# Four column tiles per unit of the expert layer, in one PSUM tile of two banks

## The chip, the cores and the metric

The kernel runs on one core of a Trainium2 chip. The metric is the device time of one execution in microseconds (us). The core's engines are PE (matmul; its weight loads are PEld), DVE (vector), ACT (activation functions), POOL (a second vector engine) and SP, which only issues transfers here. Each has its own queue and works through it in order.

## What is computed

Four sequences of 768 steps pass through a delta rule with 8 heads of width 48; its output, 3072 rows of 384, is the input x of an expert layer with 2048 hidden columns and a rational function in place of an activation:

```python
# delta rule, per batch and head
y[t] = q[t] @ state
state += beta[t] * outer(kn[t], v[t] - kn[t] @ state)
# expert layer on x = all heads' y, side by side
h = x @ w_in                      # [3072, 384] @ [384, 2048]
P = a0 + a1*h + a2*h*h + a3*h*h*h
Q = 1 + |b0|*|h| + |b1|*h*h
out = (P / (Q + 1e-6)) @ w_out    # [3072, 2048] @ [2048, 384]
```

w_in and w_out come as float64; the kernel converts them itself.

## The kernel before

**Stages.** The sequences are cut into 12 chunks of 64 steps (NCH). For a chunk the delta rule is turned into block matmuls over all heads: `front`, `middle`, `back` and `ahead` (lines 898 to 967) each have eight steps j, and `attention` (969) calls them for four different chunks at once, so that chunk c+1 is solved while chunk c+4 is loaded. A chunk gives 256 rows of x (64 steps of four sequences), which `tokens` (731) transposes and scales and `scalars` (757) gives its factors.

**A unit.** The expert layer takes a chunk's 256 rows against w_in in 8 units of two tiles of 128 hidden columns, 96 units in all, each with 2 x 256 = 512 numbers in each of 128 partitions. A product is made of three passes of 16-bit halves (PASSES). A unit n goes through four functions:

- `hidden` (802): 18 matmuls on PE (L810) into the PSUM tile ph. Its tag "h" in the pool ps_h has two buffers of one bank each (line 87), so that unit n+1 can be made while unit n is read.
- `numerator` (820): ACT makes a3*h + a2 (L827) and |b1*h| (L829) from ph; DVE makes u = h * that (L830), the denominator's part w (L832) and u's next step (L834), all three reading ph. L834 is the last reader of ph. ACT takes |w| (L833). In some units, by_pool (line 836), POOL adds a0 (L838).
- `quotient` (841): ACT makes 1/Q by Ln and Exp (L845, L846). DVE multiplies (L851, or L849 in by_pool units) and forms the rest for the low half (L852 and L856; in by_pool units POOL does the latter, L854). POOL writes the low half of g (L857).
- `accumulate` (860): 12 matmuls on PE (L872) add g @ w_out to two PSUM tiles po, the first eight from g's high half, the last four from the low half that POOL writes. After a chunk's last unit the result is scaled and stored.

by_pool holds for units 0, 4, 5 and 6 of chunks 2 to 10, 36 of 96.

**Order.** The loop at line 1010 calls, for each n, numerator(n), quotient(n-1), one attention step, accumulate(n-2) and hidden(n+1). The scheduler of the framework then lays the instructions out on each engine's queue by its own timeline; what stands in the queues is not the order of the calls.

**Weights.** `load_in` and `load_out` (338, 356) bring w_in and w_out in pieces through `to_f32` (318): one transfer, |.| on ACT (L325), a clamp on POOL (L326), three integer steps on DVE (L327, L334). They find one scale for each unit of two tiles. The staging tiles share the buffers of the expert layer's u, r and w (tags mu, mr, mw; three each) and of g (mg; three). Half of the weights (GRP = 4 units) are ready before the first unit, the rest is converted while the first four units run.

## Time and profile before

| | |
|---|---|
| time, median of 3 runs (lowest, highest) | 870.12 us (870.11, 876.16) |
| span of the profiled execution | 875.0 us |
| mean granted PE clock in it | 0.886 |
| busy: PE, PEld, DVE, ACT, POOL | 629.4, 494.5, 797.9, 550.9, 469.5 us |
| instructions | 23209 |
| first numerator step (L830) | at 151.9 us |
| L830 of the first unit of chunks 2, 9, 10, 11 | at 307.0, 745.4, 790.6, 831.7 us |

The profile is of one execution, whose span is 875.0 us, 4.9 us over the median of the runs. A row of a group gives line, engine, operation, output and inputs by tile names, shapes, count, then busy time in all and the mean of one in ns, then the engine's idle time ahead of them and what ended it. A row of the timeline begins with the start and the duration in us. On DVE an instruction's duration reaches into the next one's start by some 0.08 us, so that what it costs the queue is the time from start to start.

### The profile page before, as it was taken

Reading aid. Unit: us, or ns where it says so; the run is one execution under the profiler, and the core shown is the slowest. Engines: PE = TensorE matmul, PEld = TensorE weight load, DVE = VectorE, ACT = ScalarE, POOL = GpSimd, SP = SyncE. Lnnn points to the kernel's source line nnn. Section 1 sums busy time; section 2 is a strip of 40 time slices with the busy share of each in tenths; the row PEclk is TensorE's granted clock in tenths of the full one; section 3 lists DMA queues with packets and bytes.
Section 4 is the critical chain, followed back from the end, with each engine's and each line's share of the span. In section 5 each row is a group of like instructions: output and inputs, shape, how many; then the busy total and the mean of one; then the engine's idle time right before and its main releaser. Section 6 shows DMA issues by size and latency. Waiting matters only on the chain. (4 is left out here: it accounts for less than half of the span.)

```text
span 875.0 us, 23209 instructions
## 1 busy us (share of the span) xinstructions
PE 629.4 (72%) x9264; PEld 494.5 (57%) x9264; DVE 797.9 (91%) x1561; ACT 550.9 (63%) x1025; POOL 469.5 (54%) x430
## 2 busy tenths in 40 slices
PE   0230444875787688698778879788788878898885
PEld 0120344664565576576556667666566657676553
DVE  5999899899999789999989999999999898898996
ACT  4765675656466386585566678567576664868574
POOL 7655664537236447656646755654756444363622
PEclk9755556886999799899989989999999998999998
DMA  8987986679965987988689489597683824300000
GB/s 236 247 185 156 224 175 111 122 132 168 177 121 93 180 142 131 182 142 162 118 155 170 82 162 152 90 194 116 128 172 63 166 46 65 68 1 19 1 19 18
DMA packets 466507, 111.46 MB, mean 127 GB/s; under 512 B 431328, under 2 KB 463072, under 8 KB 466400
## 3 DMA queue, kind: packets, MB, share of 16 engines
q1 hardware_dynamic: 464224, 108.83, 66.8%
q8 instruction: 72, 1.18, 0.6%
q10 hardware_dynamic: 2176, 1.17, 0.4%
q14 instruction: 35, 0.29, 0.1%
HBM read 40.47 MB, written 26.23 MB: 76 GB/s over the span
## 5 line engine op out<-in xcount | busy, mean ns | idle before, releaser
L872 PE MATMUL po<-w_out,mg 128*128 128x384 f16 x1152 | 220.6, 339 | 42.2 <-POOL mg L857 33.7
L810 PE MATMUL ph<-xT,w_in 128*128 128x256 f16 x1728 | 221.5, 283 | 33.3 <-DVE mu L834 30.2
L810 PEld LDWEIGHTS <-w_in 128*128 128x128 f16 x1728 | 172.6, 102 | 70.5 <-DVE mu L834 22.4
L857 POOL TENSOR_TENSOR mg<-mu,mr 128x512 f16<-128x512 f32 x96 | 131.9, 1374 | 107.8 <-DVE mu L856 52.5
L872 PEld LDWEIGHTS <-mg 128*128 128x128 f16 x1152 | 109.7, 101 | 118.1 <-POOL mg L857 42.8
L827 ACT ACTIVATE mu<-ph,coef,msc 128x512 f32<-128x512 f32 x96 | 74.1, 772 | 50.4 <-POOL mg L857 17.3
L833 ACT ACTIVATE mw<-mw 128x512 f32<-128x512 f32 x96 | 60.3, 630 | 64.0 <-DVE mw L832 63.7
L852 DVE SCALAR_TENSOR_TENSOR mw<-mw,msc,mg 128x512 f32<-128x512 f32 x96 | 88.4, 922 | 0.4
L410 PEld LDWEIGHTS <-kbd 128*128 128x128 f16 x1680 | 61.7, 105 | 38.8 <-issue 36.2
L830 DVE TENSOR_TENSOR mu<-ph,mu 128x512 f32<-128x512 f32 x96 | 65.5, 683 | 17.1 <-ACT mr L829 13.4
L854 POOL TENSOR_TENSOR mu<-mu,mw 128x512 f32<-128x512 f32 x36 | 50.1, 1390 | 54.3 <-DVE mw L852 30.8
L832 DVE SCALAR_TENSOR_TENSOR mw<-mr,msc,ph 128x512 f32<-128x512 f32 x96 | 70.6, 736 | 0.0
L410 PE MATMUL pu<-z,ebd 128*128 128x48 f16 x1728 | 56.5, 188 | 19.4 <-DVE z L234 11.8
L834 DVE SCALAR_TENSOR_TENSOR mu<-mu,msc,ph 128x512 f32<-128x512 f32 x96 | 70.4, 733 | 0.0
L845 ACT ACTIVATE mr<-mw,msc 128x512 f32<-128x512 f32 x96 | 69.0, 720 | 1.8
L410 PEld LDWEIGHTS <-ebd 128*128 128x128 f16 x1728 | 55.3, 100 | 22.4 <-issue 20.9
L829 ACT ACTIVATE mr<-ph,msc 128x512 f32<-128x512 f32 x96 | 65.4, 681 | 0.0
L851 DVE SCALAR_TENSOR_TENSOR mg<-mu,msc,mr 128x512 f16<-128x512 f32 x60 | 61.5, 1024 | 2.3 <-ACT mr L846 2.3
L838 POOL TENSOR_SCALAR mu<-mu,msc 128x512 f32<-128x512 f32 x36 | 31.3, 869 | 56.3 <-DVE mu L834 50.2
L846 ACT ACTIVATE mr<-mr 128x512 f32<-128x512 f32 x96 | 60.2, 628 | 1.2
L856 DVE SCALAR_TENSOR_TENSOR mu<-mu,msc,mw 128x512 f32<-128x512 f32 x60 | 57.6, 960 | 0.2
L232 POOL TENSOR_TENSOR mm<-m,mm 128x1024 f16<-128x1024 f32 x12 | 30.3, 2527 | 44.2 <-ACT mm L228 36.0
(201 smaller groups left out, 1295.9 us busy)
## 6 DMA issues: line engine op xcount, KB each, us to landing
wsi<-in_moe_w_in_dram SPq DMA_DIRECT2D x24, 256.0 KB, 5.2
xdk<-kn SPq DMA_DIRECT2D x24, 256.0 KB, 3.6
kbd<-tk SPq DMA_DIRECT2D x24, 256.0 KB, 5.4
gd<-g SPq DMA_DIRECT2D x24, 256.0 KB, 3.4
wso<-in_moe_w_out_dram SPq DMA_DIRECT2D x32, 192.0 KB, 4.1
xdq<-kn SPq DMA_DIRECT2D x24, 256.0 KB, 3.4
mbd<-mm SPq DMA_DIRECT2D x24, 256.0 KB, 5.0
wc<-img SPq DMA_DIRECT2D x24, 256.0 KB, 4.9
```

Of the source, the lines that this page charges most:

```text
L410: nc.tensor.matmul(dst[p][:, h], head(bd, lp, p * H + h), head(rt, rp, p * H + h), start=start and n == 0 and h == 0, stop=stop and n == l ...
L810: nc.tensor.matmul(ph[:, i], w_in[:, f2, wp, cc, i * P : (i + 1) * P], x[:, xp, cc], start=k == 0, stop=k == 3 * NCC - 1,)
L827: nc.scalar.activation(u, ph, AF.Identity, scale=A3, bias=a2)
L829: nc.scalar.activation(z, ph, AF.Abs, scale=B1)
L830: nc.vector.tensor_mul(u, ph, u)
L832: nc.vector.scalar_tensor_tensor(out=w, in0=z, scalar=B0, in1=ph, op0=ALU.add, op1=ALU.mult)
L834: nc.vector.scalar_tensor_tensor(out=u, in0=u, scalar=A1, in1=ph, op0=ALU.add, op1=ALU.mult)
L845: nc.scalar.activation(r, w, AF.Ln, bias=Q0)
L851: nc.vector.scalar_tensor_tensor(out=g[:, 0], in0=u, scalar=A0, in1=r, op0=ALU.add, op1=ALU.mult)
L852: nc.vector.scalar_tensor_tensor(out=w, in0=w, scalar=Q0, in1=g[:, 0], op0=ALU.add, op1=ALU.mult)
L857: nc.gpsimd.tensor_mul(g[:, 1], u, r)
L872: nc.tensor.matmul(po[p], g[:, gp, i, p * P : (p + 1) * P], w_out[:, f2, wp, i], start=f2 == lo and i == 0 and k == 0, stop=f2 == hi - 1 a ...
```

## The change

A unit takes four tiles of 128 columns (FT = 4): a chunk has 4 units, 48 in all, and each instruction of `numerator` and `quotient` covers 1024 numbers in each partition instead of 512. `hidden` issues 36 matmuls and `accumulate` 24. The tile ph now takes two banks, and its tag has one buffer. The working tiles are twice as long; mu and mr keep three buffers, mw and mg have two. by_pool holds for units 0 and 2 of 4 in chunks 2 to 10. The attention keeps its eight steps (NS), two to a unit. The weights have one scale for four tiles, and w_in comes in 12 pieces of 512 columns instead of 24 of 256; w_out's pieces stay as they are. GRP is half of the units as before, now 2. Room in SBUF comes from a zero tile of half the length, written to each image buffer by two transfers instead of one, from the fewer buffers and from a smaller scratch area for DMA descriptors.

```diff
-    MB = 3
+    FT = 4
+    NS = 8
+    MB = {"mu": 3, "mr": 3, "mw": 2, "mg": 2}
...
-    ps_h = ctx.enter_context(tc.tile_pool(name="ps_h", bufs=2, space=PSUM))
+    ps_h = ctx.enter_context(tc.tile_pool(name="ps_h", bufs=1, space=PSUM))
...
-    zero = sb.tile([P, BS], F32, tag="ob", name="zero", bufs=1)
+    zero = sb.tile([P, BS // 2], F32, tag="ob", name="zero", bufs=1)
...
-        nc.scalar.dma_start(out=t, in_=zero)
+        for half in range(2):
+            nc.scalar.dma_start(out=t[:, half * (BS // 2) : (half + 1) * (BS // 2)], in_=zero)
...
-    NU = NF // 2
-    w_in = cpool.tile([P, NU, 2, NCC, 2 * P], F16, name="w_in")
-    w_out = cpool.tile([P, NU, 2, 2, DM], F16, name="w_out")
+    NU = NF // FT
+    w_in = cpool.tile([P, NU, 2, NCC, FT * P], F16, name="w_in")
+    w_out = cpool.tile([P, NU, 2, FT, DM], F16, name="w_out")
...
-            to_f32(t[:, cc], w64[cc * P : (cc + 1) * P, i * 4 * P : (i + 1) * 4 * P], f"i{i}_{cc}")
+            to_f32(t[:, cc], w64[cc * P : (cc + 1) * P, i * 2 * FT * P : (i + 1) * 2 * FT * P], f"i{i}_{cc}")
...
-        ph = ps_h.tile([P, 2, TG], F32, tag="h", name=f"ph_{n}")
-        for i in range(2):
+        ph = ps_h.tile([P, FT, TG], F32, tag="h", name=f"ph_{n}")
+        for i in range(FT):
...
-        u = sb.tile([P, 2, TG], F32, tag="mu", name=f"mu{n}", bufs=MB)
+        u = sb.tile([P, FT, TG], F32, tag="mu", name=f"mu{n}", bufs=MB["mu"])
...
-        w = sb.tile([P, 2, TG], F32, tag="mw", name=f"mw{n}", bufs=MB)
+        w = sb.tile([P, FT, TG], F32, tag="mw", name=f"mw{n}", bufs=MB["mw"])
...
-        by_pool = 2 <= c < NCH - 1 and f2 in (0, 4, 5, 6)
+        by_pool = 2 <= c < NCH - 1 and f2 in (0, 2)
...
-        g = sb.tile([P, 2, 2, TG], F16, tag="mg", name=f"mg{n}", bufs=MB)
+        g = sb.tile([P, 2, FT, TG], F16, tag="mg", name=f"mg{n}", bufs=MB["mg"])
...
-    GRP = 4
+    GRP = NU // 2
...
-        attention(*divmod(n + SHIFT, NU))
+        for j in range(NS // NU):
+            attention(*divmod(n * NS // NU + j + SHIFT, NS))
...
-    nc = _bacc.Bacc("TRN2", target_bir_lowering=False, num_devices=1)
+    nc = _bacc.Bacc("TRN2", target_bir_lowering=False, num_devices=1, dynamic_dma_scratch_size=1024)
```

In the changed kernel the lines of the expert layer stand seven further down: L830, L832 and L834 are L837, L839 and L841; L851, L852 and L856 are L858, L859 and L863; L849, L854 and L857 are L856, L861 and L864; L810 is L817, L872 is L879.

The scheduler lays the queues out anew. In the middle of the program, DVE's queue of the kernel before has this in chunk 5, where the third and the fourth unit of the chunk meet (mu, mw, mg and ph are the tiles u, w, g and the product of a unit; z is a step of the attention's solve, xs and px belong to `tokens`):

```order
L830 TENSOR_TENSOR mu_8536<-ph_8517,mu_8536 128x512
L832 SCALAR_TENSOR_TENSOR mw_8541<-mr_8538,msc_7531,ph_8517 128x512
L745 TENSOR_REDUCE xs_8554<-px_8557 1x1
L856 SCALAR_TENSOR_TENSOR mu_8422<-mu_8422,msc_7531,mw_8427 128x512
L834 SCALAR_TENSOR_TENSOR mu_8536<-mu_8536,msc_7531,ph_8517 128x512
L830 TENSOR_TENSOR mu_8606<-ph_8587,mu_8606 128x512
L832 SCALAR_TENSOR_TENSOR mw_8611<-mr_8608,msc_7531,ph_8587 128x512
L234 SCALAR_TENSOR_TENSOR z_1_8960<-pu_8699,zmask,z_1_8960 128x768
L747 TENSOR_SCALAR xs_8554<-px_8557 128x1
L834 SCALAR_TENSOR_TENSOR mu_8606<-mu_8606,msc_7531,ph_8587 128x512
```

The changed kernel has this in chunk 5, from the second numerator to the third:

```order
L837 TENSOR_TENSOR mu_7650<-ph_7613,mu_7650 128x1024
L839 SCALAR_TENSOR_TENSOR mw_7655<-mr_7652,msc_6979,ph_7613 128x1024
L670 TENSOR_TENSOR m_8_7564<-pm_7515,mask 128x1024
L237 SCALAR_TENSOR_TENSOR z_0_8166<-pu_8108,zmask,z_0_8166 128x768
L841 SCALAR_TENSOR_TENSOR mu_7650<-mu_7650,msc_6979,ph_7613 128x1024
L752 TENSOR_REDUCE xs_7980<-px_7983 1x1
L858 SCALAR_TENSOR_TENSOR mg_7974<-mu_7650,msc_6979,mr_7652 128x1024
L859 SCALAR_TENSOR_TENSOR mw_7655<-mw_7655,msc_6979,mg_7974 128x1024
L237 SCALAR_TENSOR_TENSOR z_1_8352<-pu_8108,zmask,z_1_8352 128x768
L863 SCALAR_TENSOR_TENSOR mu_7650<-mu_7650,msc_6979,mw_7655 128x1024
L754 TENSOR_SCALAR xs_7980<-px_7983 128x1
L837 TENSOR_TENSOR mu_7962<-ph_7925,mu_7962 128x1024
```

Before, the numerators of two units stand next to each other, and the quotient of a unit falls in among the next one's numerator. Now a unit's quotient follows its own numerator, and between L841 and the next L837 stand its three steps, one split of 768 columns and two short ones.

At the end of the program, in chunk 11, where the attention is over, DVE's queue had this:

```order
L830 TENSOR_TENSOR mu_13826<-ph_13807,mu_13826 128x512
L832 SCALAR_TENSOR_TENSOR mw_13831<-mr_13828,msc_13599,ph_13807 128x512
L851 SCALAR_TENSOR_TENSOR mg_13837<-mu_13774,msc_13599,mr_13776 128x512
L834 SCALAR_TENSOR_TENSOR mu_13826<-mu_13826,msc_13599,ph_13807 128x512
L852 SCALAR_TENSOR_TENSOR mw_13779<-mw_13779,msc_13599,mg_13837 128x512
L830 TENSOR_TENSOR mu_13875<-ph_13856,mu_13875 128x512
L856 SCALAR_TENSOR_TENSOR mu_13774<-mu_13774,msc_13599,mw_13779 128x512
```

and has this in the changed kernel:

```order
L837 TENSOR_TENSOR mu_12769<-ph_12732,mu_12769 128x1024
L839 SCALAR_TENSOR_TENSOR mw_12774<-mr_12771,msc_12627,ph_12732 128x1024
L841 SCALAR_TENSOR_TENSOR mu_12769<-mu_12769,msc_12627,ph_12732 128x1024
L858 SCALAR_TENSOR_TENSOR mg_12857<-mu_12769,msc_12627,mr_12771 128x1024
L859 SCALAR_TENSOR_TENSOR mw_12774<-mw_12774,msc_12627,mg_12857 128x1024
L863 SCALAR_TENSOR_TENSOR mu_12769<-mu_12769,msc_12627,mw_12774 128x1024
L837 TENSOR_TENSOR mu_12846<-ph_12809,mu_12846 128x1024
```

The quotient of the unit before, which stood among a numerator's steps, is gone from there; nothing but the unit's own quotient stands between two numerators.

40 lines of the change are left out of this document (22 added, 18 removed).

## The prediction

> **What bounds the kernel now.** I read the busy shares first, then the busy time by stage, then the groups of instructions, then who waited for whom.
>
> ```profile
> PE 629.4 (72%) x9264; PEld 494.5 (57%) x9264; DVE 797.9 (91%) x1561; ACT 550.9 (63%) x1025; POOL 469.5 (54%) x430
> ...
> 0.00:152.00 152.00, 46.20 (x731) 39.72 (x731) 133.90 (x365) 92.01 (x235) 92.62 (x129) 0.66 0.87 192
> 152.00:307.00 155.00, 114.27 (x1760) 90.05 (x1761) 137.31 (x274) 87.78 (x155) 72.06 (x57) 0.87 0.82 141
> 307.00:745.00 438.00, 361.71 (x5691) 286.94 (x5688) 413.13 (x737) 282.68 (x488) 253.74 (x203) 0.94 0.74 132
> 745.00:831.00 86.00, 76.09 (x886) 57.70 (x881) 79.46 (x140) 61.99 (x108) 40.16 (x33) 1.00 0.12 23
> 831.00:875.00 44.00, 31.11 (x208) 20.07 (x208) 34.13 (x48) 26.39 (x44) 10.94 (x9) 0.94 0.07 18
> ```
>
> The columns of the stages are PE, PEld, DVE, ACT and POOL busy. The cuts are the first numerator (152) and the first numerator of chunks 2, 9 and 11. DVE is busy 91% of the span and 94% (413.13 of 438) in the long middle, where PE is at 83%. So DVE sets the pace, with PE not far behind. What it does:
>
> ```profile
> L830 DVE TENSOR_TENSOR mu<-ph,mu 128x512 f32<-128x512 f32 x96 | 65.5, 683 | 17.1 <-ACT mr L829 13.4 <-POOL mg L857 1.6 <-POOL nrm L504 1.2
> L832 DVE SCALAR_TENSOR_TENSOR mw<-mr,msc,ph 128x512 f32<-128x512 f32 x96 | 70.6, 736 | 0.0
> L834 DVE SCALAR_TENSOR_TENSOR mu<-mu,msc,ph 128x512 f32<-128x512 f32 x96 | 70.4, 733 | 0.0
> L852 DVE SCALAR_TENSOR_TENSOR mw<-mw,msc,mg 128x512 f32<-128x512 f32 x96 | 88.4, 922 | 0.4
> L851 DVE SCALAR_TENSOR_TENSOR mg<-mu,msc,mr 128x512 f16<-128x512 f32 x60 | 61.5, 1024 | 2.3 <-ACT mr L846 2.3
> L856 DVE SCALAR_TENSOR_TENSOR mu<-mu,msc,mw 128x512 f32<-128x512 f32 x60 | 57.6, 960 | 0.2
> L849 DVE TENSOR_TENSOR mg<-mu,mr 128x512 f16<-128x512 f32 x36 | 31.3, 868 | 4.4 <-ACT mr L846 3.1 <-POOL mu L838 1.4
> ...
> L857 POOL TENSOR_TENSOR mg<-mu,mr 128x512 f16<-128x512 f32 x96 | 131.9, 1374 | 107.8 <-DVE mu L856 52.5 <-ACT mr L846 7.2 <-ACT sq L242 7.0
> L854 POOL TENSOR_TENSOR mu<-mu,mw 128x512 f32<-128x512 f32 x36 | 50.1, 1390 | 54.3 <-DVE mw L852 30.8 <-PE ph L810 3.4 <-ACT mr L845 3.2
> L838 POOL TENSOR_SCALAR mu<-mu,msc 128x512 f32<-128x512 f32 x36 | 31.3, 869 | 56.3 <-DVE mu L834 50.2 <-DVE sf L253 3.7 <-DVE xs L747 2.3
> ```
>
> The seven expert groups are 445 us, over half of DVE's time. DVE's one steady wait in them is L830, 17.1 us in all.
>
> **The fixed part of an instruction.** 96 old units become 48 new ones, and every instruction of a unit runs once over 1024 columns instead of twice over 512. What a merge saves is read from starts that follow each other without a wait:
>
> ```profile
> 859.52 0.68 DVE L830 TENSOR_TENSOR mu<-ph,mu 128x512 f32<-128x512 f32 x1
> 860.12 0.74 DVE L832 SCALAR_TENSOR_TENSOR mw<-mr,msc,ph 128x512 f32<-128x512 f32 x1
> 860.78 0.81 DVE L851 SCALAR_TENSOR_TENSOR mg<-mu,msc,mr 128x512 f16<-128x512 f32 x1
> ...
> 66.91 1.21 DVE L663 TENSOR_TENSOR m<-pm,mask 128x1024 f32<-128x1024 f32 x1
> 68.05 0.13 DVE L253 TENSOR_SCALAR sw<-lgw 128x1 uint32<-128x1 uint32 x1
> ...
> 602.16 1.00 DVE L234 SCALAR_TENSOR_TENSOR xT<-px,sf,xT 128x768 f16<-128x768 f32 x1
> 603.09 0.56 DVE L770 TENSOR_SCALAR kp<-kp,coef 128x1 f32<-128x1 f32 x3
> ```
>
> A two-input product takes 0.60 us from start to start at 512 columns and 1.14 at 1024 (L663, which already reads two banks of PSUM at once), so a merge saves 0.06. The three-operand form takes 0.66 at 512 and 0.93 at 768; the slope makes 1.20 at 1024, so a merge saves 0.12. Merges: 48 of L830 and 18 of L849 at 0.06 (4.0 us); 48 each of L832, L834, L852 and 30 each of L851 and L856 at 0.12 (24.5 us). **DVE's work shrinks by 28.5 us.** Ends: all 270 merges at 0.06 give 16; at 0.15 (twice 683 less L663's 1.21, by durations) 41. ACT and POOL save as well, but neither sets the pace. POOL's share stays (2 of 4 new units where 4 of 8 old ones were). Two buffers of mw and mg in place of three cost nothing: the work of two new units lies between two uses of a buffer, as that of three old ones did, and w and g are done within one and a half. No product, no byte and no weight load goes away on PE.
>
> **The conversion of the weights.** w_in arrives in 12 pieces, not 24, of three DVE instructions each: 36 go, at 0.06 to 0.12. Four of eight column scales go too. That is 3 to 5 us of a stage in which DVE is busy 133.90 of 152. Against it the first piece is twice as long, and DVE stands waiting for it:
>
> ```profile
> 18.38 0.47 DVE L327 TENSOR_SCALAR w_out<-wai 128x256 uint32<-128x256 uint32 x1 [4.72 <-POOL wai L326]
> ```
>
> The image buffers are zeroed by four DMAs, not two, on ACT's queue:
>
> ```profile
> 9.09 1.00 ACTq L206 DMA_DIRECT2D img<-zero  x2
> ```
>
> That is 1 us more of issuing there; ACT then waits for DVE anyway. I take **-2.5 us**, ends -5 and 0.
>
> **The lock between DVE and POOL.** Two instructions that start together show it:
>
> ```profile
> 616.88 1.27 POOL L854 TENSOR_TENSOR mu<-mu,mw 128x512 f32<-128x512 f32 x1
> 616.89 1.81 DVE L852 SCALAR_TENSOR_TENSOR mw<-mw,msc,mg 128x512 f32<-128x512 f32 x1
> ```
>
> DVE, reading two SBUF tiles, ends 0.55 us after POOL does: it stood until POOL was through. Over their undisturbed 0.68 to 0.75 us, the four groups L852, L851, L856 and L849 lost 17, 17, 13 and 7 us that way. Merged, such meetings are half as many and twice as long: no change. But the attention instructions on DVE, as many as before, now meet POOL instructions of about 2.4 us, where 1.27 stood. Those of 64 columns show the size:
>
> ```profile
> L576 DVE TENSOR_TENSOR pr<-ab,wt 128x64 f32<-128x64 f32 x24 | 11.5, 516 | 0.1
> L571 DVE TENSOR_TENSOR pr<-gb,wt 128x64 f32<-128x64 f32 x24 | 8.0, 368 | 0.1
> ...
> 628.14 0.23 DVE L571 TENSOR_TENSOR pr<-gb,wt 128x64 f32<-128x64 f32 x1
> ```
>
> Against 0.23 undisturbed these two lost 10 us, and POOL's expert work is about 45% of its busy time. I take **+7 us**, ends 0 (POOL's starts fall into DVE's longer PSUM reads, which hold nothing) and +20 (all such waits double). The Trainium skill (SBUF — State Buffer, "Who interferes with whom") says that a Vector instruction with two SBUF inputs contends with a GpSimd instruction that reads SBUF, and that the loser stands for the whole instruction. By that rule, the trace agrees; it is what makes the third rival possible.
>
> **One tile in place of two.** The tag h had two buffers of one bank; it has one of two banks. So hidden(n+1) may start only when L834 of unit n has read the tile, and DVE may start the next numerator only after that product and ACT's first pass. Behind the waiting product stand, on PE, unit n's accumulations and the attention groups of the next steps; DVE's splits and residuals wait for those.
>
> ```profile
> 613.68 2.12 PE L810 MATMUL ph<-xT,w_in 128*128 128x256 f16 x18 [0.47 <-DVE mu L834]
> 601.23 2.11 PE L872 MATMUL po<-w_out,mg 128*128 128x384 f16 x12
> 604.38 1.37 PE L410 MATMUL pu<-z,ebd 128*128 128x48 f16 x48
> ...
> L827 ACT ACTIVATE mu<-ph,coef,msc 128x512 f32<-128x512 f32 x96 | 74.1, 772 | 50.4 <-POOL mg L857 17.3 <-DVE msc L794 11.3 <-PE ph L810 11.0
> L526 ACT ACTIVATE g<-pg 128x1024 f32<-128x1024 f32 x12 | 12.2, 1020 | 11.3 <-PE pg L410 8.8 <-DMA knbd<-xdk 2.5
> ```
>
> The product takes 2 x 2.12 = 4.2 us. ACT's first pass over 1024 lies between 1.02 (L526) and 1.54 (twice L827); I take 1.2. So between two numerators DVE must have 5.5 us of other work, or it stands. In the middle a new unit has 438/28 = 15.6 us, of which numerators take 3.6: on average there is twice the work needed. But it is uneven. In the piece of the order of chunk 5 printed above, DVE has between L834 and the next L830 (L841 and L837 there) only three long quotient steps (1.2 each), a 768-column split (0.93) and two short ones: 4.7 us, while PE has 5.5 to do and an attention group of 1.37 in its midst. One such place in most of 7 chunks and a second in some, at 0.9 to 2.3 us, make 6 to 20 us, part of which swallows lock waits that DVE would have stood anyway. I take **+9 us**, ends 0 and +36 (each of 28 units stands for ACT's 1.2 us and a handover).
>
> **The end of the program.** Attention runs out from chunk 9 on, and with it the filling.
>
> ```profile
> 745.39 0.69 DVE L830 TENSOR_TENSOR mu<-ph,mu 128x512 f32<-128x512 f32 x1 [0.29 <-ACT mr L829]
> 790.59 0.69 DVE L830 TENSOR_TENSOR mu<-ph,mu 128x512 f32<-128x512 f32 x1 [1.55 <-ACT mr L829]
> 831.67 0.69 DVE L830 TENSOR_TENSOR mu<-ph,mu 128x512 f32<-128x512 f32 x1 [1.56 <-POOL mg L857]
> ```
>
> Two old units take 11.3 us in chunk 9 and 10.3 in chunk 10; in chunk 11 the seven steps from 831.67 to 859.52 make 8.0 for two. A new unit without attention goes round so: L834 ends; 4.2 product; 1.2 ACT; DVE 1.14 + 1.20 + 1.28; three handovers of 0.1: 9.3. PE also has the 24 accumulations of unit n between hidden(n+1) and hidden(n+2), the last eight of which need POOL's product: ACT's three passes after L839 (1.1 each, an estimate between the two rows above) end 2.3 us after L834, three DVE steps come to 5.9, POOL 2.4 to 8.3, eight matmuls (0.176 each) to 9.7. So 9.7 for a round. Chunk 11 loses three rounds of 1.7 (5 us). The last chain is longer too: from the last L830 to the end took 15.5 us (859.52 to 875); with every step over 1024 I get 19.1. Together 9 us more than measured, 11.5 against a sum that has already credited four units with 0.6 each. Chunks 9 and 10 sit at the round's limit, and give back their 5 us of credit. **+16 us**, ends +8 and +22.
>
> **The sum.** 875.0 - 28.5 - 2.5 + 7 + 9 + 16 = 876.0 us against the profiled execution's span of 875.0: +1.0. The median of the runs is 870.12, so I predict 871.0.
>
> **Rivals.** *The filling holds* (faster): lock waits and stands for the product fall on each other in the middle, so both terms are 0. For it: on average twice the needed work, and DVE waits little now (17.1 us at L830). Against: the uneven places in the order. 875.0 - 31 + 16 = 860, that is 855 at the median. A measured case in the Trainium skill (TensorE: Matmul & The Clock Gate, "HAM oscillation — how this bites in real kernels") gained nothing from a second PSUM buffer; by it this rival would win. No run here shows it yet.
>
> *Lockstep* (slower): hidden(n+1) stands behind accumulations and attention groups that wait for POOL, so DVE runs dry in each unit of the middle, not in one or two of a chunk. It decides as soon as DVE's work between two numerators falls under 5.5 us plus PE's delay. For it, with two buffers still:
>
> ```profile
> PE po L872 <- POOL mg L857: 33.7, 30, 3.9
> PE ph L810 <- DVE mu L834: 30.2, 21, 5.2
> ```
>
> Against it: PE has 17% to spare. +36 in place of +9: 871 + 27 = 898.
>
> *The longer lock* (slower): +20 in place of +7, 884.
>
> **How the numbers follow.** The forecast, gains eaten by the single tile and the tail, has 0.38; the filling holds 0.31; lockstep 0.19; the longer lock 0.12. About 1% (8.7 us) is what a measurement of this kernel can tell from no change. So faster 0.31, same 0.38, slower 0.31. The forecast's own range is 861 to 879. To hold 8 in 10, the range reaches from 849, past the first rival, to 896, just short of lockstep.
>
> **What would show it.** Right: DVE about 30 us less busy, near 774; groups of 1024 at 1.21 and 1.28; more idle time in front of the first numerator step than 17.1, most of it released by ACT or PE; new units of the last chunk 9.5 to 10 us apart. PE's wait for that step far above 30 us. Wrong if the middle is shorter than 425 us (the filling holds), if idle time before the numerator passes 40 us in the middle (lockstep), or if the 64-column groups rise past 0.6 us (lock).

## The result, and the profile after

The changed kernel is slower: 937.14 us (median of 4 runs, 936.52 to 937.97) against 873.14 us for the kernel before on the same chip, a ratio of 1.0754 with a 95% interval of 1.0694 to 1.0813 (the quotient of the two medians is 1.0733). The profiled execution's span is 935.0 us, 60.0 more than before. The prediction of 871.0 us, with a range of 849 to 896, was wrong.

First the busy times of the page:

```profile
PE 660.0 (71%) x9251; PEld 515.6 (55%) x9252; DVE 763.4 (82%) x1227; ACT 506.1 (54%) x741; POOL 449.8 (48%) x334
```

Then the busy time by stage (columns PE, PEld, DVE, ACT, POOL; the cuts are the first numerator of the program and those of chunks 1, 9 and 11):

```profile
0.00:149.40 149.40, 46.73 (x718) 38.81 (x719) 126.51 (x285) 83.21 (x182) 88.29 (x112) 0.88 0.88 193
149.40:227.30 77.90, 57.21 (x820) 45.26 (x821) 68.79 (x131) 43.41 (x69) 40.27 (x33) 0.81 0.74 133
227.30:791.50 564.20, 440.21 (x6662) 349.15 (x6661) 470.93 (x694) 302.66 (x404) 275.69 (x168) 0.88 0.73 124
791.50:882.30 90.80, 80.23 (x843) 59.98 (x842) 67.33 (x95) 55.11 (x67) 36.13 (x18) 0.94 0.07 16
882.30:935.00 52.70, 35.57 (x214) 22.39 (x212) 29.84 (x24) 21.73 (x23) 9.41 (x4) 0.86 0.06 15
```

The same cuts before were 151.9, 78.5, 515.0, 86.3 and 43.3 us. So the start (up to the first numerator) gained 2.5 us, chunk 0 gained 0.6, **chunks 1 to 8 lost 49.2**, chunks 9 and 10 lost 4.5, and chunk 11 with the end lost 9.4. DVE has 34.5 us less to do in all, and still the kernel is longer: DVE's share fell from 91% to 82%. It stands idle. The groups of DVE (after the bar: busy, mean ns, idle before and its releasers):

```profile
L841 DVE SCALAR_TENSOR_TENSOR mu<-mu,msc,ph 128x1024 f32<-128x1024 f32 x48 | 61.0, 1271 | 0.0
...
L837 DVE TENSOR_TENSOR mu<-ph,mu 128x1024 f32<-128x1024 f32 x48 | 58.5, 1219 | 39.0 <-ACT mr L836 39.0
L858 DVE SCALAR_TENSOR_TENSOR mg<-mu,msc,mr 128x1024 f16<-128x1024 f32 x30 | 46.3, 1542 | 22.9 <-ACT mr L853 21.6 <-POOL nrm L511 1.1
...
L856 DVE TENSOR_TENSOR mg<-mu,mr 128x1024 f16<-128x1024 f32 x18 | 25.5, 1415 | 13.4 <-ACT mr L853 9.0 <-issue 2.3 <-PE po L879 1.6
...
L583 DVE TENSOR_TENSOR pr<-ab,wt 128x64 f32<-128x64 f32 x24 | 8.5, 396 | 0.2
...
L578 DVE TENSOR_TENSOR pr<-gb,wt 128x64 f32<-128x64 f32 x24 | 4.3, 221 | 0.3
```

The merged steps last what was forecast (1.219 and 1.271 us). The 64-column groups, which were to show a longer lock, became shorter (0.396 and 0.221 us where 0.516 and 0.368 stood). The idle time is new: 39.0 us before the numerator's first step (17.1 before), and 36.3 before the first step of the quotient (L856 and L858), where 6.8 stood. The waits across engines say the same:

```profile
ACT mu L834 <- PE ph L817: 81.8, 34, 5.4
...
PE ph L817 <- DVE mu L841: 38.5, 14, 8.9
...
DVE mg L858 <- ACT mr L853: 21.6, 13, 2.8
DVE z L237 <- ACT z L233: 15.3, 10, 5.0
```

ACT's wait for the product rose from 11.0 to 81.8 us. One round of the last chunk, where no attention work is left, shows who waits in what order (the rows of ACT and DVE, start and duration first):

```profile
892.97 1.10 ACT L836 ACTIVATE mr<-ph,msc 128x1024 f32<-128x1024 f32 x1
894.11 1.23 DVE L837 TENSOR_TENSOR mu<-ph,mu 128x1024 f32<-128x1024 f32 x1 [1.98 <-ACT mr L836]
895.25 1.27 DVE L839 SCALAR_TENSOR_TENSOR mw<-mr,msc,ph 128x1024 f32<-128x1024 f32 x1
896.44 1.28 DVE L841 SCALAR_TENSOR_TENSOR mu<-mu,msc,ph 128x1024 f32<-128x1024 f32 x1
896.56 1.06 ACT L840 ACTIVATE mw<-mw 128x1024 f32<-128x1024 f32 x1 [2.48 <-DVE mw L839]
897.64 1.15 ACT L852 ACTIVATE mr<-mw,msc 128x1024 f32<-128x1024 f32 x1
898.83 1.06 ACT L853 ACTIVATE mr<-mr 128x1024 f32<-128x1024 f32 x1
899.97 1.28 DVE L858 SCALAR_TENSOR_TENSOR mg<-mu,msc,mr 128x1024 f16<-128x1024 f32 x1 [2.26 <-ACT mr L853]
901.29 1.28 DVE L859 SCALAR_TENSOR_TENSOR mw<-mw,msc,mg 128x1024 f32<-128x1024 f32 x1
901.98 1.20 ACT L834 ACTIVATE mu<-ph,coef,msc 128x1024 f32<-128x1024 f32 x1 [2.09 <-PE ph L817]
902.61 1.28 DVE L863 SCALAR_TENSOR_TENSOR mu<-mu,msc,mw 128x1024 f32<-128x1024 f32 x1
903.08 1.10 ACT L836 ACTIVATE mr<-ph,msc 128x1024 f32<-128x1024 f32 x1
904.22 1.22 DVE L837 TENSOR_TENSOR mu<-ph,mu 128x1024 f32<-128x1024 f32 x1 [0.32 <-ACT mr L836]
```

After L841 DVE stands 2.26 us until ACT has made absolute value, logarithm and exponential. With two tiles the next numerator stood in that gap. Then DVE does the quotient while PE makes the product, and it stands again before the next L837 if the product is late. Before, the two waits covered each other's work; now they follow one another. L837 reads what ACT's first pass, L834, wrote (ended at 903.18), and yet it starts only after the second one, L836 (ended at 904.18). It is so in all 48 units of this trace: L837 never starts before L836 has ended, and in 24 of them it starts less than 0.15 us after. In the middle the gaps are filled with attention work, but not reliably:

```profile
557.24 4.74 PE L817 MATMUL ph<-xT,w_in 128*128 128x256 f16 x36
...
565.42 1.34 ACT L231 CAST mm<-m 128x1024 f16<-128x1024 f32 x1 [7.02 <-DMA mbd<-mm]
566.62 1.19 ACT L834 ACTIVATE mu<-ph,coef,msc 128x1024 f32<-128x1024 f32 x1
567.71 1.10 ACT L836 ACTIVATE mr<-ph,msc 128x1024 f32<-128x1024 f32 x1
568.80 0.90 ACT L233 ACTIVATE z<-pu,zmask 128x768 f16<-128x768 f32 x1
568.85 1.22 DVE L837 TENSOR_TENSOR mu<-ph,mu 128x1024 f32<-128x1024 f32 x1 [6.36 <-ACT mr L836]
```

Here the product is ready at 562.0, but on ACT's queue the first pass over it stands behind an attention cast that waits 7.02 us for a transfer; DVE stands 6.36 us, the longest of its waits for L837 in the whole trace.

### The profile page after: what moved, and what is told of

It is laid out like the page before. It is cut to its first block, busy times and chain, and to the rows that moved or that the text cites. A ratio compares the mean times of both kernels' runs of the same rounds, so it can differ in the third digit from the quotient of the medians.

```text
span 935.0 us, 22261 instructions
## 1 busy us (share of the span) xinstructions
PE 660.0 (71%) x9251; PEld 515.6 (55%) x9252; DVE 763.4 (82%) x1227; ACT 506.1 (54%) x741; POOL 449.8 (48%) x334
## 4 chain that ended last, share of the span: by engine, by line
DVE 29%; PE 22%; DMA 16%; SPq 11%; ACT 10%; issue 7%; POOL 5%; POOLq 0%; ACTq 0%; DVEq 0%
PE ph L817 9%; PE po L879 7%; DVE mw L839 2%; DVE mu L837 2%; DVE mg L858 2%; DVE w_out L337 2%; SPq L623 2%; DVE mw L859 2%; PE pu L417 2%; SPq L121 2%; DVE pr L566 2%; DMA xdq<-kn 2%; DMA tk<-xdk 2%; ACT mr L836 2%; ACT mu L834 2%
## 5 line engine op out<-in xcount | busy, mean ns | idle before, releaser
L817 PE MATMUL ph<-xT,w_in 128*128 128x256 f16 x1728 | 225.7, 292 | 41.2 <-DVE mu L841 38.5
L879 PE MATMUL po<-w_out,mg 128*128 128x384 f16 x1152 | 221.1, 349 | 41.4 <-ACT ob L893 19.1
L817 PEld LDWEIGHTS <-w_in 128*128 128x128 f16 x1728 | 178.5, 105 | 77.6 <-issue 25.0
L879 PEld LDWEIGHTS <-mg 128*128 128x128 f16 x1152 | 115.7, 104 | 124.7 <-issue 40.0
L864 POOL TENSOR_TENSOR mg<-mu,mr 128x1024 f16<-128x1024 f32 x48 | 114.6, 2388 | 129.1 <-DVE mu L863 116.0
L834 ACT ACTIVATE mu<-ph,coef,msc 128x1024 f32<-128x1024 f32 x48 | 57.8, 1203 | 85.7 <-PE ph L817 81.8
L840 ACT ACTIVATE mw<-mw 128x1024 f32<-128x1024 f32 x48 | 50.7, 1056 | 96.6 <-DVE mw L839 96.5
L837 DVE TENSOR_TENSOR mu<-ph,mu 128x1024 f32<-128x1024 f32 x48 | 58.5, 1219 | 39.0 <-ACT mr L836 39.0
L417 PEld LDWEIGHTS <-kbd 128*128 128x128 f16 x1680 | 67.7, 106 | 22.3 <-issue 16.7
L859 DVE SCALAR_TENSOR_TENSOR mw<-mw,msc,mg 128x1024 f32<-128x1024 f32 x48 | 68.0, 1417 | 0.6
L861 POOL TENSOR_TENSOR mu<-mu,mw 128x1024 f32<-128x1024 f32 x18 | 43.8, 2433 | 49.2 <-DVE mw L859 42.3
L858 DVE SCALAR_TENSOR_TENSOR mg<-mu,msc,mr 128x1024 f16<-128x1024 f32 x30 | 46.3, 1542 | 22.9 <-ACT mr L853 21.6
L841 DVE SCALAR_TENSOR_TENSOR mu<-mu,msc,ph 128x1024 f32<-128x1024 f32 x48 | 61.0, 1271 | 0.0
L839 DVE SCALAR_TENSOR_TENSOR mw<-mr,msc,ph 128x1024 f32<-128x1024 f32 x48 | 61.0, 1271 | 0.0
L852 ACT ACTIVATE mr<-mw,msc 128x1024 f32<-128x1024 f32 x48 | 55.0, 1146 | 1.2
L836 ACT ACTIVATE mr<-ph,msc 128x1024 f32<-128x1024 f32 x48 | 53.0, 1105 | 0.0
L235 POOL TENSOR_TENSOR mm<-m,mm 128x1024 f16<-128x1024 f32 x12 | 29.5, 2460 | 46.9 <-ACT mm L231 46.9
L853 ACT ACTIVATE mr<-mr 128x1024 f32<-128x1024 f32 x48 | 50.6, 1054 | 1.0
L237 DVE SCALAR_TENSOR_TENSOR z<-pu,zmask,z 128x768 f16<-128x768 f32 x36 | 36.4, 1011 | 15.4 <-ACT z L233 15.3
```

The costliest lines, as they stand in the source:

```text
L417: nc.tensor.matmul(dst[p][:, h], head(bd, lp, p * H + h), head(rt, rp, p * H + h), start=start and n == 0 and h == 0, stop=stop and n == l ...
L817: nc.tensor.matmul(ph[:, i], w_in[:, f2, wp, cc, i * P : (i + 1) * P], x[:, xp, cc], start=k == 0, stop=k == 3 * NCC - 1,)
L834: nc.scalar.activation(u, ph, AF.Identity, scale=A3, bias=a2)
L836: nc.scalar.activation(z, ph, AF.Abs, scale=B1)
L837: nc.vector.tensor_mul(u, ph, u)
L839: nc.vector.scalar_tensor_tensor(out=w, in0=z, scalar=B0, in1=ph, op0=ALU.add, op1=ALU.mult)
```

## The experiments

In all eighteen kernels the scheduler lays the queues out anew. How much that alone moves is shown by b_pairs, b_bufs and b_combo, which take no work away and of which the third holds the edits of the other two: 0.9926, 0.9956 and 1.0001, so some 0.7% or 6 us. Differences smaller than that are not read as effects. The ratios are against the kernel before on the same chip.

| kernel | us | ratio, 95% interval |
|---|---|---|
| b_onetile | 941.80 | 1.0795 (1.0758 to 1.0833) |
| b_pairs | 865.06 | 0.9926 (0.9891 to 0.9961) |
| a_halves | 914.10 | 1.0491 (1.0439 to 1.0542) |
| a_spread | 941.98 | 1.0799 (1.0756 to 1.0842) |
| a_actshort | 903.08 | 1.0361 (1.0313 to 1.0409) |
| a_short | 920.05 | 1.0558 (1.0499 to 1.0617) |
| a_short_onetile | 950.84 | 1.0905 (1.0838 to 1.0972) |
| b_bufs | 866.55 | 0.9956 (0.9926 to 0.9985) |
| b_grouped | 897.56 | 1.0339 (1.0284 to 1.0393) |
| a_woven | 895.52 | 1.0282 (1.0243 to 1.0321) |
| b_combo | 871.43 | 1.0001 (0.9976 to 1.0027) |
| b_cut | 874.75 | 1.0039 (1.0015 to 1.0064) |
| a_cut | 893.80 | 1.0260 (1.0219 to 1.0301) |
| b_noln | 874.19 | 1.0032 (1.0003 to 1.0061) |
| a_noln | 922.11 | 1.0581 (1.0538 to 1.0624) |
| b_cutacc | 867.37 | 0.9959 (0.9935 to 0.9982) |
| a_cutacc | 917.90 | 1.0542 (1.0479 to 1.0605) |
| a_cut_noln | 879.61 | 1.0110 (1.0063 to 1.0158) |

For the two kernels and fourteen of the others I added up DVE's idle gaps from the trace by the step that ended them: the numerator's first step, the quotient's first step, and everything else (attention, tokens, weights), in us of the profiled execution.

```
                 span   DVE busy | numerator  quotient  others
before           875.0   797.9   |   17.1        6.8      44.3
after            935.0   763.4   |   39.0       36.3      86.1
b_onetile        940.8   777.8   |   35.9       69.9      47.2
a_halves         910.3   789.4   |   28.4       19.5      61.0
a_actshort       897.7   783.7   |   18.0       16.3      69.6
a_short          914.1   809.7   |   23.1        8.1      64.9
a_short_onetile  949.9   807.2   |   64.6        6.9      60.8
b_grouped        892.4   815.1   |   21.7        6.9      39.9
a_woven          895.0   784.0   |   23.5       11.0      65.4
b_cut            870.8   803.2   |   13.2        7.3      39.1
a_cut            891.6   763.4   |   12.1       15.7      90.4
b_noln           872.1   785.1   |   17.9        9.3      50.3
a_noln           918.8   771.1   |   44.3       14.4      78.7
a_cut_noln       878.2   766.8   |   16.6        5.7      79.1
b_cutacc         867.2   797.4   |   16.3        7.6      37.3
a_cutacc         910.6   756.8   |   36.5       31.3      74.7
```

The first two rows are the account of the result: 34.5 us less work, 21.9 more idle time before the numerator, 29.5 before the quotient, 41.8 before other steps. (The last column is some 37, 46, 44 and 92 us in b_pairs, b_bufs, b_combo and a_spread.)

The stages tell more. In chunks 1 to 8, which lost 49.2 us, the three columns went from 8.8, 4.5 and 21.2 us to 23.1, 14.6 and 57.1. So there most of the new idle time, 35.9 us, stands before the other steps, while two thirds of the new time before the quotient, 19.4 us, stands from chunk 9 on.

**One tile, or the attention in lumps?** The theory after the result was the single tile; the rivals were attention steps that now come two at a time, and steps of twice the length.

```diff
# b_onetile, against the kernel before
-    ps_h = ctx.enter_context(tc.tile_pool(name="ps_h", bufs=2, space=PSUM))
+    ps_h = ctx.enter_context(tc.tile_pool(name="ps_h", bufs=1, space=PSUM))
```

> The kernel before, units of two column tiles, with one buffer of one bank for the product in place of two; nothing else is changed. One-tile theory (the changed kernel loses its 64 us because a product may start only after the last reader of the one before, and DVE the next numerator only after that product and ACT's first pass): here a product takes 2.1 us and ACT's pass 0.8, against about 5.9 us of other DVE work per unit in the middle, so nearly the same shortage as in the changed kernel; slower by 25 to 60 us, idle time before the numerator's first step from 17 to over 40 us. Lumps theory (two attention steps per unit arrive together and the in-order queues stand behind their late inputs): within 10 us of the kernel before. Long-steps theory (each instruction of 1024 holds its queue longer, so every hand-over between ACT, DVE, POOL and PE comes later): within 15 us.

It took 941.8 us, 70 more than before and more than the 25 to 60 expected, and with no other change. The idle time before the numerator, 35.9 us, stayed under the 40 expected. Its rows of DVE, against 17.1 and 2.3 us of idle time at the same lines before:

```profile
L830 DVE TENSOR_TENSOR mu<-ph,mu 128x512 f32<-128x512 f32 x96 | 65.6, 683 | 35.9 <-ACT mr L829 33.6 <-ACT sf L789 1.0 <-POOL nrm L504 0.3
L851 DVE SCALAR_TENSOR_TENSOR mg<-mu,msc,mr 128x512 f16<-128x512 f32 x60 | 52.2, 871 | 41.3 <-ACT mr L846 41.1
```

Most of the new idle time stands before the quotient, not before the numerator. That is the wait that the prediction did not have in the middle: with one tile the next numerator has no product yet when DVE has done a unit's numerator, so it cannot fill the time in which ACT prepares the quotient.

```diff
# b_pairs, against the kernel before
-        attention(*divmod(n + SHIFT, NU))
+        for j in range(2 if n % 2 == 0 else 0):
+            attention(*divmod(n + j + SHIFT, NU))
# a_spread, against the changed kernel
+        attention(*divmod(n * NS // NU + SHIFT, NS))
         if 0 <= n - 1 < N:
             quotient(n - 1)
-        for j in range(NS // NU):
-            attention(*divmod(n * NS // NU + j + SHIFT, NS))
         if 0 <= n - 2 < N:
             accumulate(n - 2)
+        attention(*divmod(n * NS // NU + 1 + SHIFT, NS))
```

> The kernel before with the attention steps called two at a time at every second unit, as the changed kernel calls them; units, tiles and buffers as before. Lumps theory: slower by 25 us or more. One-tile theory and long-steps theory: within 9 us of the kernel before (1%).

> The changed kernel with the two attention steps of a unit called apart, one between the numerator and the quotient of the unit before, the other after the accumulation; nothing else is changed. Lumps theory: faster than the changed kernel by 20 us or more. One-tile theory: 925 to 950 us, no gain. Long-steps theory: the same, no gain.

Attention in pairs costs nothing (865.06 us), and spreading it brings nothing back (941.98). The lumps are out.

```diff
# a_halves, against the changed kernel
-    ps_h = ctx.enter_context(tc.tile_pool(name="ps_h", bufs=1, space=PSUM))
+    ps_h = ctx.enter_context(tc.tile_pool(name="ps_h", bufs=2, space=PSUM))
...
-        nc.vector.tensor_mul(u, ph, u)
+        for i, p2 in enumerate(ph):
+            h2 = slice(2 * i, 2 * i + 2)
...
+            nc.vector.tensor_mul(u[:, h2], p2, u[:, h2])
```

> The changed kernel with the product in two tiles of one bank each (two buffers); ACT's two passes and DVE's three steps that read the product run once for each half, all other steps over 1024 as in the changed kernel. DVE keeps 126 of its 270 merges, worth 13 us. One-tile theory: the loss goes, and 855 to 885 us. Lumps theory: 920 to 945, the tile was not the cause. Long-steps theory: in between, 890 to 920, since the quotient, ACT's logarithm and exponential and POOL's product still run over 1024.

914.10 us: the second tile, bought back with 144 unmerged DVE steps, recovers 23 us, and 43 stay. The one-tile theory expected 855 to 885 and is not the whole cause; the time lies in the range of the long-steps theory, 890 to 920, which a_short tests next.

**What stays with two tiles.**

```diff
# a_actshort, against a_halves (the same for logarithm and exponential)
+            nc.scalar.activation(w[:, h2], w[:, h2], AF.Abs)
-        nc.scalar.activation(w, w, AF.Abs)
# a_short, against a_actshort
+        for i in range(2):
+            h2 = slice(2 * i, 2 * i + 2)
+            ui, wi, ri, gh, gl = u[:, h2], w[:, h2], r[:, h2], g[:, 0, h2], g[:, 1, h2]
...
-        nc.gpsimd.tensor_mul(g[:, 1], u, r)
+            nc.gpsimd.tensor_mul(gl, ui, ri)
# a_short_onetile, against a_short
-    ps_h = ctx.enter_context(tc.tile_pool(name="ps_h", bufs=2, space=PSUM))
+    ps_h = ctx.enter_context(tc.tile_pool(name="ps_h", bufs=1, space=PSUM))
...
+        pt = ps_h.tile([P, FT, TG], F32, tag="h", name=f"ph_{n}")
+        ph = [pt[:, 0:2], pt[:, 2:4]]
# b_bufs, against the kernel before (mw and mg, the weights' staging with them)
+    MB2 = 2
```

> The changed kernel with the product in two tiles of one bank each and, beyond that, ACT's three passes between numerator and quotient (absolute value, logarithm, exponential) run once for each half. DVE's and POOL's quotient steps still run over 1024. Long-chain theory (what is left of the loss once there are two tiles, 43 us, comes from dependent steps of twice the length, ACT's three passes of 1.1 us above all): 885 to 903 us, and DVE's idle time before the quotient under 10 us where the two-tile kernel had 19.5. Grouping theory (the rest comes from the unit of four itself: attention, accumulations and g's two buffers in lumps of twice the size): 905 to 925 us.

> The changed kernel with the product in two tiles of one bank each and every step of numerator and quotient, on ACT, DVE and POOL, run once for each half; units of four, their accumulations, their buffers and the order of the calls stay as in the changed kernel. All 270 merges are given back, so DVE's work is about that of the kernel before. Long-chain theory: 860 to 882 us, as the kernel before. Grouping theory: 910 to 935 us, the loss stays and the 13 us of the last merges come on top.

> The changed kernel with its one tile of two banks, but every step of numerator and quotient run once for each half of 512. Beside the kernel with short steps and two tiles it tells what one tile costs when the steps are short and the unit is long. Filling theory (with one tile DVE cannot run the next numerator while ACT makes absolute value, logarithm and exponential of the unit before): 15 to 40 us above the kernel with short steps and two tiles, the second half's numerator fills a part. If the cost is that of the unit's round through PE alone, as large as with units of two: 60 us or more above it. If long steps are what makes one tile costly: within 9 us of it.

> The kernel before with two buffers of mw and of mg in place of three, nothing else. The prediction held this to cost nothing: within 9 us of the kernel before. Fewer-buffers theory (a unit's denominator and its g must be through before the second next may start, and that costs the changed kernel its two-tile rest of 43 us): slower by 20 us or more.

a_short, with DVE's work as before and every step short, took 920.05 us: the long-chain theory fell, and the unit of four costs 49 us even with two tiles and short steps. Merging the quotient on DVE and POOL is worth 17 us of that (a_actshort, 903.08), merging ACT's three passes between numerator and quotient costs 11 (a_halves against a_actshort). a_actshort lies on the border of both expectations, and its idle time before the quotient, 16.3 us, not under 10, speaks against the long chain too. Two buffers of mw and mg cost nothing. One tile costs 31 us with short steps, in the range of the filling theory, but the idle time stands before the numerator there (64.6 against 23.1), and not before the quotient:

```profile
L841 DVE TENSOR_TENSOR mu<-ph,mu 128x512 f32<-128x512 f32 x96 | 65.7, 684 | 64.6 <-ACT mr L840 64.4
...
L866 DVE SCALAR_TENSOR_TENSOR mg<-mu,msc,mr 128x512 f16<-128x512 f32 x60 | 51.4, 858 | 3.3 <-ACT mr L862 3.2
```

This fits the view that within such a unit the second half's numerator covers ACT's passes for the first, so that only the round through PE is left; no run tests that by itself.

**Is it the order of the calls?**

```diff
# b_grouped, against the kernel before
+    for n in range(0, N + 4, 2):
+        for i in range(2):
+            if n < N:
+                numerator(n + i)
+        for i in range(2):
+            if 0 <= n - 2 < N:
+                quotient(n - 2 + i)
...
+            attention(*divmod(n + i + SHIFT, NU))
...
+                accumulate(n - 4 + i)
...
+                hidden(n + 2 + i)
# a_woven, against a_actshort: m counts halves, n, h = divmod(m, 2)
+    for m in range(2 * N + 3):
+        if m < 2 * N:
+            numerator(m)
+        if m % 2 == 0 and 2 <= m < 2 * N + 2:
+            quotient(m // 2 - 1)
+        attention(*divmod(m + SHIFT, NS))
+        if 0 <= m - 3 < 2 * N:
+            accumulate(m - 3)
...
+        if m + 1 < 2 * N:
+            hidden(m + 1)
# b_combo, against the kernel before: the edits of b_pairs and b_bufs, the half zero tile and
+    nc = _bacc.Bacc("TRN2", target_bir_lowering=False, num_devices=1, dynamic_dma_scratch_size=1024)
```

> The kernel before with everything called in twos, as a unit of four calls it: two numerators, two quotients (of the two units before), two attention steps, two accumulations (of the two units before those), two products. Units, tiles and steps stay at two column tiles; mu and mr have six buffers and mw and mg four, which is the room of the changed kernel, with its half-size zero tile and its smaller descriptor area. Grouping-of-calls theory (what is left of the loss with two tiles, 43 to 49 us, comes from the order in which the work is called: products of 36 matmuls and accumulations of 24 at a stretch on PE, two quotients late, so that the attention's links and the expert layer wait for each other's longer turns): 895 to 925 us. Tile-grain theory (it comes from tiles of 1024 that are filled, waited for and freed as a whole): 860 to 882 us.

> The changed kernel with the product in two tiles of one bank, ACT's three passes in halves, and every call but the quotient made by half units in the order of the kernel before: numerator of a half, (every second time) the quotient of the unit before, one attention step, accumulation of a half, product of a half. DVE's and POOL's quotient steps run over 1024, which keeps 126 of the 270 merges on DVE, 13 us. Grouping-of-calls theory: 850 to 872 us, the loss goes and the merges that are left show. Tile-grain theory: 890 to 910 us, as the same kernel with whole calls (903).

> The kernel before with four side parts of the change at once: attention steps called in pairs, two buffers of mw and mg, zero tile of half the length, smaller descriptor area. All theories now alive: none of these costs anything, 855 to 872 us; the pairs alone gave 865 and the buffers alone 867. If the smaller descriptor area slows the transfers, which the chain of waits of the changed kernel would allow (DMA 16%, SP's queue 11% of it): 885 us or more.

In the small unit it costs time; that a_short lost its time in this way is not shown. Calling small units in twos costs 26 us by medians (897.56), over half of what a_short lost and in the range of the grouping theory. The idle table shows how: DVE stands no longer than before, it is busy 17.2 us more. Its quotient steps meet POOL more: of the 96 instructions of the step below, 55 overlap an instruction of POOL on the timeline, for 58.4 us, where 46 did before, for 38.5 us. The row is b_grouped's (L852 had 88.4 us and 922 ns before):

```profile
L854 DVE SCALAR_TENSOR_TENSOR mw<-mw,msc,mg 128x512 f32<-128x512 f32 x96 | 101.6, 1061 | 0.8
```

But this is not where a_short lost its time. Chunks 1 to 8 took 553.9 us in a_short and 516.2 in b_grouped; the kernel before took 515.0 there, and b_pairs, b_bufs and b_combo 502.6 to 504.5. Most of b_grouped's loss stands from chunk 9 on (145.2 us against 129.6). And weaving the calls back into half units brought the unit of four only from 903 to 895.5 us, hardly more than the scatter, where the grouping theory had 850 to 872 and the tile-grain theory 890 to 910. Its steps other than numerator and quotient wait 65.4 us, as in all kernels with the long unit (61 to 92) and in none with the short one (37 to 50). That fits tiles of the long unit that are filled and freed as a whole; but the quotient stays whole in a_woven too, and no run separates the two. The side parts together cost nothing (b_combo).

**Through what does the single tile cost?** Each cut is made in both kernels, and the gap between the two is compared with the uncut 64.0 us.

```diff
# b_cut, a_cut
-                for wp, xp in PASSES:
+                for wp, xp in PASSES[:1]:
# b_noln, a_noln
-        nc.scalar.activation(r, w, AF.Ln, bias=Q0)
-        nc.scalar.activation(r, r, AF.Exp, scale=-1.0)
+        nc.scalar.activation(r, r, AF.Copy, scale=2.0 ** -30)
# b_cutacc, a_cutacc
-        for k, (gp, wp) in enumerate(sorted(PASSES)):
+        for k, (gp, wp) in enumerate(sorted(PASSES)[2:]):
# a_cut_noln: the first two together
```

> The kernel before with only one of the three passes of the product h = x @ w_in (12 matmuls per unit of four tiles' worth in place of 36, 6 in place of 18 per unit), so its output is not the full product's. Only a base for the changed kernel cut in the same way. DVE sets the pace and its work stays, so 830 to 868 us.

> The changed kernel with only one of the three passes of the product, 12 matmuls of 0.117 us (1.4 us) where 36 took 4.2. Round-through-the-product theory (the term of the prediction, only undersized: DVE waits for the product and ACT's first pass after it): the gap to the kernel before that is cut in the same way falls from 64 us to under 20. Ordering theory (with one tile the next numerator cannot fill DVE's wait for ACT's absolute value, logarithm and exponential, and longer turns of a unit of four hold up the attention's links): the gap stays above 40.

> The kernel before with logarithm and exponential, two ACT passes of 0.6 us per unit, replaced by one scaled copy that does not depend on the denominator, so that 1/Q is left out of the output. Only a base for the changed kernel without them. DVE's work stays: 840 to 870 us.

> The changed kernel with logarithm and exponential, two dependent ACT passes of 1.1 us per unit after the absolute value, replaced by one scaled copy that does not depend on the denominator (1/Q is left out of the output). Filling theory (with one tile DVE has to stand for ACT's three passes before the quotient): the gap to the kernel before without them falls from 64 us to 20 to 40, by the 29 us of idle time that the changed kernel has more before the quotient. Round-through-the-product theory: the gap stays above 50.

> The kernel before with only the last of the three passes of the accumulation g @ w_out, the one that reads g's low half from POOL (4 matmuls in place of 12 per unit); its output lacks the other passes. Only a base for the changed kernel cut in the same way: 850 to 878 us.

> The changed kernel with only the last of the three passes of the accumulation, 8 matmuls in place of 24: as much time is taken off PE per unit (2.8 us) as by cutting the product, but none off the way from the last reader of the tile through the product to the next numerator. If the product's place in that way is what counts: the gap to the kernel before cut in the same way stays above 45 us, where the cut product left 19. If it is only PE's load, as the longer turns on its queue: the gap falls under 30 as it did there.

> The changed kernel with both cuts: one of three passes of the product, and one scaled copy in place of logarithm and exponential. Its base is the kernel before with either cut, both 874 to 875 us. If the two causes are apart, 45 us by the product and 16 by ACT's passes, the gap goes: 870 to 882 us. If they are two views of the same wait: 888 to 896 us, as with the cut product alone.

| cut | before, cut | changed, cut | gap, us | difference of the ratios |
|---|---|---|---|---|
| none | 873.14 | 937.14 | 64.0 | 0.075 (±0.006) |
| product, 36 to 12 matmuls | 874.75 | 893.80 | 19.1 | 0.022 (±0.005) |
| logarithm and exponential | 874.19 | 922.11 | 47.9 | 0.055 (±0.005) |
| accumulation, 24 to 8 matmuls | 867.37 | 917.90 | 50.5 | 0.058 (±0.007) |
| product, logarithm, exponential | 874.5 (mean of the two) | 879.61 | 5.1 | 0.007 (±0.005) |

(The bounds are worked out from the two intervals. The kernel before was not run with both cuts; its base in the last row is the mean of the two single ones.) The kernel before gains nothing from any cut of PE's or ACT's work that is larger than the scatter, so neither engine is its bound. The changed kernel gains 43 us from a shorter product, and the gap closes by 45, as the round-through-the-product theory expected. As many microseconds of matmuls taken off PE at the accumulation close it by only 13.5 us (50.5 left, above the 45 named). Leaving out logarithm and exponential closes it by 16; the 47.9 us left lie between the two expectations and confirm neither, and 16 can hardly be told from the accumulation's 13.5. With both cuts 5 us are left, as if the two added up.

By these totals the product's **place** counts, between the last reader of the tile and the next numerator. By stage it looks otherwise. These are the gaps between the two profiled executions, us:

| cut | start and chunk 0 | chunks 1 to 8 | chunk 9 to the end |
|---|---|---|---|
| none | -3.1 | 49.2 | 13.9 |
| product | -0.4 | 25.0 | -3.7 |
| logarithm and exponential | 6.1 | 30.9 | 9.7 |
| accumulation | 6.8 | 18.3 | 18.4 |

From chunk 9 on, where the attention's work runs out, the shorter product closes the gap and the shorter accumulation does not: there its place is what counts. In chunks 1 to 8, where most of the time was lost, the accumulation's cut closes the gap as well as the product's; the difference of 6.7 us is within what the order alone moved in that stage (502.6 to 515.0 us in the kernel before and its three neutral variants). So for the middle the product's place is not shown, and a part of the loss there can be PE's load. The accumulation is not a clean counterpart either: with it cut, a matmul of the product took 301 ns on average, where it took 292.

In the groups of a_cut the idle time before numerator and quotient falls together:

```profile
L837 DVE TENSOR_TENSOR mu<-ph,mu 128x1024 f32<-128x1024 f32 x48 | 58.4, 1217 | 12.1 <-ACT mr L836 10.9 <-ACT lgx L270 1.1
L858 DVE SCALAR_TENSOR_TENSOR mg<-mu,msc,mr 128x1024 f16<-128x1024 f32 x30 | 45.0, 1501 | 10.6 <-ACT mr L853 10.5
```

In a_noln only the second does (L857 is the quotient's first step there). In a_cutacc neither does over the whole program: before the numerator it falls from 23.1 to 12.6 us in chunks 1 to 8 and rises from 14.1 to 22.3 from chunk 9 on.

```profile
L837 DVE TENSOR_TENSOR mu<-ph,mu 128x1024 f32<-128x1024 f32 x48 | 58.6, 1220 | 44.3 <-ACT mr L836 41.7 <-PE po L878 2.3
L857 DVE SCALAR_TENSOR_TENSOR mg<-mu,msc,mr 128x1024 f16<-128x1024 f32 x30 | 48.6, 1618 | 7.4 <-ACT mr L852 6.4 <-ACT lgx L270 0.8
```

```profile
L837 DVE TENSOR_TENSOR mu<-ph,mu 128x1024 f32<-128x1024 f32 x48 | 58.4, 1216 | 36.5 <-ACT mr L836 36.5
L858 DVE SCALAR_TENSOR_TENSOR mg<-mu,msc,mr 128x1024 f16<-128x1024 f32 x30 | 45.6, 1519 | 23.7 <-ACT mr L853 23.4
```

Even so a_cut_noln is no faster than the kernel before, though DVE has 31.1 us less to do in it. What eats that is the third column: 79.1 us of idle time before other steps, where 39 to 50 stood. No run took this away. It is spread over many waits (before splits, norms, masks and scalars of the attention), and through which link of the attention it arises stays open.

## Why the prediction was wrong

- **DVE bounds the kernel, and merges save a fixed part.** Right. The groups came out at 1.219 and 1.271 us (1.21 and 1.28 named). The first numerator came 2.5 us earlier, as forecast for the weights.
- **The lock, +7 us.** Too high, not too low. DVE's busy time was named as 774 us and is 763.4; the attention's 64-column steps got faster. A DVE that stands more meets POOL less: b_onetile, with the same instructions as before, is busy 20 us less, and 61 of its 252 quotient steps overlap an instruction of POOL, where 131 did before. Where the order of the calls alone changed (b_grouped), DVE was busy 17 us more, 12 of them in the quotient steps that meet POOL. The rival of the longer lock is out.
- **One tile in place of two, +9 us. This step failed.** The prediction put it so: between two numerators "DVE must have 5.5 us of other work, or it stands", and "on average there is twice the work needed". It saw that on PE the attention's groups stand behind the waiting product, and that "DVE's splits and residuals wait for those", but gave that no cost. Chunks 1 to 8 should have come out about 3 us shorter (19 us of merges, less 7 and 9) and came out 49.2 longer. Idle time before the numerator, the one place that the term priced, grew by 14.3 us there; before the quotient it grew by 10.1, and before the other steps, most of them the attention's, by 35.9. The tile itself costs 70 us in the small unit and 31 in the long unit with short steps; a second tile in the changed kernel brings back 23 of the 64 us. Four things were missing:
  1. The quotient was counted as work at hand, while it stands behind ACT's three passes over its own unit, 3.3 us after L839: 29.5 us of new idle time in all. The prediction used these passes for the end of the program and left them out of the middle.
  2. The round is longer than 5.5 us even with the product at its fastest: the shortest stretch from the end of L841 to the next L837 is 6.50 us (897.72 to 904.22 above), since L837 starts only after ACT's second pass, and the prediction counted the first alone, though its row of L830 names the second (L829) as what DVE waited for. Why DVE waits for it, no run shows.
  3. The product did not take 4.2 us each time after PE had stood, but up to 6.2 (below).
  4. The other work is not ready when it is wanted: ACT's first pass stood behind a late attention input in the piece at 557 to 569 us, and DVE waited 15.3 us in all for ACT's step z of the solve.

  An average of work over time says nothing about that. Through which link most of the 35.9 us come about stays open.
- **The end, +16 us.** Too low, but within its ends: with the credit of the merges it meant +9 for the last three chunks, and 13.9 was measured, which makes the term 21. The rounds of the last chunk were 11.8, 10.1 and 11.7 us, not 9.7. Each had ACT's second pass in it, the product was slow in two of them (5.77 and 4.77 us), and in the last it also started some 1 us after L841, behind accumulations.
- **Two buffers of mw and mg at no cost.** Right (b_bufs, 0.9956).
- **The unit of four as a whole** was costed at nothing and costs 49 us with two tiles and short steps (a_short). Through what is not shown: the order of the calls alone costs 26 us in the small unit, but at another place of the program.
- **The rivals.** Lockstep (898) had the mechanism, DVE dry behind the product, but priced it at 36 us, where chunks 1 to 8 lost 49 with the merges' gain already in it, and its sign was in the wrong place: idle time before the numerator was 39.0 us in all and 23.1 in chunks 1 to 8, not over 40; the greater part stood before the quotient and before the attention's steps. PE's wait for the last numerator step, which was to be far above 30 us, was 38.5. "The filling holds" rested on a measured case of the Trainium skill (TensorE: Matmul & The Clock Gate, "HAM oscillation — how this bites in real kernels") in which a second PSUM buffer gained nothing. It does not carry over: here the second buffer alone is worth 70 us of 942.

No version came out that is clearly faster than the kernel before. b_pairs (0.9926) and b_bufs (0.9956) lie below it, but both edits together gave 1.0001, so I take these for the scatter of the scheduler's orders.

## What to carry to other kernels

Before giving up a second buffer for longer instructions, write down the whole round of one buffer (last reader, producer, first pass, next reader) and go through what the bounding engine has *ready* at each wait in it, its own unit's later steps included; do not set an average of other work against it. A merge that saves 0.06 to 0.12 us per instruction is small beside the loss of one overlap per unit, and of what else the longer unit holds up, which came to over 1 us per unit here (64 us over 48 units, the merges' gain already in it). To find through which link a round costs, shorten one link in both kernels and compare the gaps, with a cut of the same size outside the round beside it, and do so stage by stage: here the totals set the two cuts far apart, and the long middle did not.
